# Scores of keys ahead of scores of queries in the first chunk of a delta-rule attention with a feed-forward block

## The chip, the core and the metric

The kernel runs on one core of a Trainium2 chip. The core has TensorE (PE; its loading of weights is listed as PEld), VectorE (DVE), ScalarE (ACT), GpSimd (POOL) and SyncE (SP), which issues all of this kernel's DMAs. The metric is the time of one execution on the device in microseconds. Before the change it is 787.22 us, the median of three runs (784.6, 787.22, 788.08).

## What is computed

A delta-rule attention over 4 batches, 8 heads, 768 steps and a head dimension of 48, and then a feed-forward block with SiLU on the 3072 tokens:

```python
k_n = k / (np.linalg.norm(k, axis=-1, keepdims=True) + 1e-06)
for t in range(S):
    y[:, :, t] = np.einsum('bhd,bhde->bhe', q[:, :, t], state)
    v_old = np.einsum('bhde,bhd->bhe', state, kt)
    state = state + bt[:, :, :, None] * np.einsum('bhd,bhe->bhde', kt, vt - v_old)
...
h = x @ w_in                              # x: the attention's output, (3072, 384); w_in: (384, 2048)
g = h * (1.0 / (1.0 + np.exp(-h)))
out = g @ w_out                           # w_out: (2048, 384)
```

The weights come as 64-bit floats and are made into 32-bit floats on the chip.

## The kernel before, in words

The 768 steps are cut into six chunks of 128. A unit is one batch of one chunk, with all 8 heads; each chunk has four units. Within a chunk the recurrence is written as a triangular system: the scores between the keys, times the step sizes, form a triangular matrix per head, and its inverse gives the values that are really added to the state.

For one chunk, the steps are these. `squares` and `norms` (L284, L301) make the step sizes g from the norms of the keys and beta. `turn` (L353) transposes k and q of a unit on PE into the tile kq; ACT copies the transposes from PSUM (L371 for k, L369 for q, with a factor of -1). `score` (L376) multiplies the transposed keys with keys and queries together (L387, 256 columns: 128 of keys and 128 of queries). The results go into the tile ap, scaled by g; the part of the queries is also masked with the triangle `above`. ACT evicts some heads (L397), DVE the others together with the mask (L403). `block_out` (L415) writes the 32 x 32 diagonal blocks of the key scores to DRAM with four DMAs per unit, and `block_in` (L435) reads them back with one head's block per partition, into the tile g. `invert` (L441) is the substitution: DVE makes the inverses of all 128 blocks, one row after another, by pairs of instructions at L465 and L469, each of which reads two SBUF tiles. When it is done (L473 on ACT, L474 on DVE), the blocks go out to DRAM as `up` and `low` (L480) and come back in pieces (L490). `solve` (L508) merges the blocks (`merge`, L540, evicted at L548, L549 and L545, L546), applies them to the values (L572, L580; sums at L563, copies at L590, L595), updates the state and makes the attention's output xT (L650, L662). `feed_forward` (L867) then runs over the chunk: `hidden` (L720) with w_in, `project` (L744) or, from the second chunk on, `combine` (L806) with w_out.

The first chunk, chunk 0, has no feed-forward work to lie beside it. In its place the weights are made narrow: `narrow` (L150) takes a piece of 768 KB and needs two ACT instructions (L158, L163), three DVE instructions (L160, L166, L170) and an addition on POOL (L174). `fetch_w_in` (L192) and `fetch_w_out` (L219) load the pieces. `fill(n)` (L936) emits the next n steps of this, in a fixed queue: eight pieces of w_in, then eight of w_out. `busy` (L261) emits matmuls whose result nobody uses.

The order on each engine is the order in which the program emits instructions: `pin` (L88) ties each instruction to the one before it on its engine, and `in_line` (L98) does the same for the DMAs of SP's queue. So an instruction that waits holds up all that follow on its engine. PSUM has three pools, psA and psC with three banks and psM with two.

The part that the change touches is L142 to L145 (first loads: beta, k of the four units, q of the four units), and L878 to L1007 (the written-out order of chunk 0). There, before the change, q is loaded behind k; `turn` and `score` of each unit run whole, one unit after another; POOL makes bkb (L340) and, after the substitution, scales the values (L348). While DVE does the substitution (the loop at L959), beta of the other chunks is transposed, the loads named in `ORDER` are emitted, k and q of chunk 1 are transposed at the steps named in `TURN`, and 20 `busy` follow. After the loop the loads of `REST` are emitted, `squares(1)` and `norms(1)`, then `fill(3)`, and the solve of chunk 0 begins, with some `busy` behind its first steps.

Of the kernel before, what the change touches and what calls it, by code (L numbers as in the profile page):

```python
# [10 lines left out]
FP32 = mybir.dt.float32  # L11
# [10 lines left out]
def kernel(  # L22
# [51 lines left out]
    def bank(pool, tag, name):  # L74
        return pool.tile([P, 512], FP32, name=name, tag=tag)
# [22 lines left out]
    def in_line(dma):  # L98

        if line:  # L100
            behind(dma, line[-1])
        line.append(dma)
        return dma
# [36 lines left out]
    pin(nc.vector.memset(states[B - 1][:], 0.0))  # L140
    beta_fm = mlp.tile([BH, S], FP32, name="beta_fm", tag="gT", bufs=3)
    in_line(nc.sync.dma_start(out=beta_fm[:], in_=beta.rearrange("b h s -> (b h) s")))  # L142
    for load_one in (load_k, load_q):
        for i in range(B):
            load_one(i)  # L145
    w_in = const.tile([P, NKT, DFF], FP32, name="w_in")
    HFF = NFF // 2
    w_outs = [const.tile([P, HFF, DM], FP32, name=f"w_out{i}") for i in range(2)]
# [43 lines left out]
    def fetch_w_in(i):  # L192
        if i < 4:
            raw = room(1 - i // 2, i % 2)
        elif i < NWI - 1:
            raw = mlp.tile([P, SIZE], U32, name="raw", tag="gT", bufs=3)[:]
        else:
            raw = spare
        raw = raw.rearrange("p (a f) -> p a f", a=NKT)
        src = moe_w_in.rearrange("(a p) f -> p a f", p=P)[:, :, i * WF : (i + 1) * WF].bitcast(U32)  # L200
        in_line(nc.sync.dma_start(out=raw, in_=src))
        raws["in", i] = raw.rearrange("p a (f j) -> p a f j", j=2)
# [58 lines left out]
    def busy(after=None, how=NoSync):  # L261

        pw = bank(psC, "c", "pw")
        done = pin(nc.tensor.matmul(
            pw[:, 0:DM], lhsT=ident[:],
            rhs=states[B - 1][:].rearrange("p a w -> p (a w)")[:, 0:DM], start=True, stop=True,
        ))
        if after is not None:
            behind(done, after, how)
        return done  # L270
# [13 lines left out]
    def squares(c):  # L284

        sums[c] = small.tile([P, BH], FP32, name="ss", bufs=1)[:]
        for b in range(B):
            if c == 1:
                sq = packed(zbufs[b])
            else:  # L290
                if b % HB == 0:
                    two = work.tile([P, HB, H, D], FP32, name="sq", tag="g" if c > 0 else "xg"[b // HB], bufs=1)
                sq = two[:, b % HB]
            pin(nc.scalar.activation(
                out=sq, in_=packed(kbufs[(c * B + b) % NK]), func=ACTF.Square
            ))
            pin(nc.vector.tensor_reduce(
                out=sums[c][:, b * H : (b + 1) * H], in_=sq, axis=AX.X, op=ALU.add
            ))
# [53 lines left out]
    def turn(i, *rooms):  # L353

        b, c = units[i]
        kb, qb = kbufs[i % NK], zbufs[i % NZ]
        kq = work.tile([P, NP, 2, C], FP32, name="kq", bufs=4)
        u = dict(kq=kq, bkb=bkbufs[i % NBK])
        for j, (src, room) in enumerate(zip((kb, qb), rooms)):
            if j == 1:  # L360
                yield u
            pt = bank(*room, "pt")
            for p in range(NP):
                pin(nc.tensor.transpose(  # L364
                    pt[:, p * C : (p + 1) * C], src[:, p].rearrange("p e w -> p (e w)"), ident[:]
                ))
            ptv = pt[:].rearrange("p (a t) -> p a t", a=NP)
            if j == 1:
                pin(nc.scalar.mul(kq[:, :, j, :], ptv, -1.0))  # L369
            elif c <= 1:  # L370
                pin(nc.scalar.copy(kq[:, :, j, :], ptv))  # L371
            else:
                pin(nc.vector.tensor_copy(out=kq[:, :, j, :], in_=ptv))
        yield u

    def score(i, u, rooms):  # L376
# [5 lines left out]
        for g, room in enumerate(rooms):  # L382
# [29 lines left out]
            u["ends"] = (copied, masked)  # L412
            yield

    def block_out(i, u):  # L415

        b, c = units[i]
        ap = u["ap"]
        if b == 0:
            blocks[c] = (  # L420
                tc.dram_tile([B, H, NB, T, T], FP32, name=f"blocks{c}"),
                work.tile([P, T, T], FP32, name="g", tag="g", bufs=1),
                work.tile([P, T, T], FP32, name="x", tag="x", bufs=1),
            )
            x = blocks[c][2]
            pin(nc.gpsimd.memset(x[:], 0.0))  # L426
            pin(nc.gpsimd.memset(x[:].rearrange("p s t -> p (s t)")[:, 0 : T * T : T + 1], 1.0))
        there = blocks[c][0]
        for j in range(NB):
            rows = slice(T * j, T * (j + 1))  # L430
            in_line(nc.sync.dma_start(  # L431
                out=there[b, :, j].rearrange("h s t -> s h t"), in_=ap[rows, :, 0, rows]
            ))

    def block_in(i):  # L435
        b, c = units[i]
        there, g, _ = blocks[c]
        rows = slice(T * b, T * (b + 1))
        in_line(nc.sync.dma_start(out=g[rows], in_=there[b].rearrange("h j s t -> (h j) s t")))

    def invert(c):  # L441

# [432 lines left out]
                yield from project(c, b, o)  # L875


    ORDER, TURN, REST = {1: (2, 3, "q", "v", 4)}, (5, 7, 9, 11), (5, 6, 7)  # L878
    A, CC, M = (psA, "a"), (psC, "c"), (psM, "m")

    def go(steps, n=1):
        for _ in range(n):
            next(steps, None)
# [19 lines left out]
    for _ in range(3):  # L903
        busy()
    squares(0)
    turning = [turn(b, M, M) for b in range(2)]
    us = [next(t) for t in turning]
    beta_of(0)
    for t in turning:
        next(t)  # L910
    norms(0)
    for b in range(B):
        if b >= 1 and b + 1 < B:
            us.append(list(turn(b + 1, M, M))[0])
        go(score(b, us[b], (CC, A)), 3)
        block_out(b, us[b])
        if b > 0:
            block_in(b - 1)
    block_in(B - 1)
    for b in range(B):  # L920
        scale(b)
    for i in range(B, 2 * B):
# [36 lines left out]
    for n, done in enumerate(invert(0)):  # L959
        if n == 1:  # L960
            for c in range(1, NCH):
                beta_of(c)
        for of in ORDER.get(n, ()):
            if of == "q":
                for i in range(B, 2 * B):
                    load_q(i)
            elif of == "v":
                for i in range(B):
                    load_v(i)
            else:  # L970
                fetch_w_in(of)
        if n in TURN:
            next_us.append(list(turn(B + len(next_us), M, M))[0])
        if n == 18:
            for i in range(20):
                busy(done if i == 0 else None, Sync)
    for i in REST:
        fetch_w_in(i)
    squares(1)
    norms(1)  # L980

    def until(piece):
        while piece is not None and piece not in narrowed:
            fill(1)
# [4 lines left out]
        fetch_w_out(i)  # L989

    fill(3)
    for i in (0, 1, 4):
        more(i, ("in", 1))
    for b in range(B):
# [2 lines left out]
    for n, _ in enumerate(solve(0, us)):  # L997
        fill(2)
        if n == 3:
            more(2)  # L1000
            more(3)
        if n == 8:
            more(5, ("out", 1))
        for _ in range((3, 3, 2, 2, 1, 1, 1)[n] if n < 7 else 0):
            busy()
        if n >= 7:
            go(pieces, 2)  # L1007
# [91 lines left out]
```

## Time and profile before

| what | number |
|---|---|
| median of three runs | 787.22 us |
| the profiled execution's own time | 784.6 us |
| its span, first to last instruction | 782.7 us |
| mean granted TensorE clock | 0.973 |
| PE busy over the span | 94% |
| DVE busy over the span | 53% |
| substitution of chunk 0 on DVE (L456 to L469) | 31.58 to 53.98 us |
| POOL's idle time ahead of L174 at 62.08 | 33.4 us |
| first matmul of the feed-forward part (L726) | 91.84 us |

A row of the timeline gives the start, the duration, the engine, the line and operation, the output and inputs with their shapes, and the number of merged instructions; in brackets stands the idle time before it and what ended that. A row of the windows gives, for a stretch, its length, the busy time of PE, PEld, DVE, ACT and POOL with the number of instructions, then the granted clock of PE, the share of the DMA engines, and GB/s. The granted clock is 1.00 or 0.50 in most stretches of the first 100 us: 1.00 from 10 to 30, 0.50 from 35 to 45, 1.00 from 50 to 75 and 0.50 from 80 to 85. A load of k or q of a unit (192 KB) takes 1.2 us of a full DMA queue, at about 163 GB/s; a piece of w_in (768 KB) 2.0 us, at about 390 GB/s.

### The profile page before, as it was taken

What the parts mean: (1) busy time and instruction counts of PE and PEld (TensorE: products, weight loads), DVE (VectorE), ACT (ScalarE), POOL (GpSimd) and SP (SyncE); (2) the same over time, 40 slices, a digit from 0 to 9 for tenths busy, and PEclk for the clock granted to TensorE, in tenths of its full rate; (3) what the DMA queues carried; (4) which work ended last, traced back from release to release, by engine and by line L of the source; (5) the groups of instructions that cost most, each with busy time, mean ns of one, the idle gap of its engine ahead of it and who ended that gap; (6) DMA issues with size and microseconds to landing.
All of it is one profiled execution on the core that took longest, in us unless ns stands there. A gap on an engine that the chain in (4) does not pass through costs nothing.

```text
span 782.7 us, 16587 instructions
## 1 busy us (share of the span) xinstructions
PE 736.8 (94%) x6806; PEld 635.1 (81%) x6806; DVE 411.9 (53%) x1050; ACT 227.3 (29%) x492; POOL 83.6 (11%) x95
## 2 busy tenths in 40 slices
PE   7389899999999799999899999899999999999998
PEld 5255786677877799988799998799998899998987
DVE  6889697852543753544572446492454592321212
ACT  6445475121233122324112315112314202212020
POOL 4006347000003000003000003000003000000000
PEclk9779899999999899999899999999999999999999
DMA  9888353130126022026213025303025203010000
GB/s 173 162 181 243 123 169 71 37 95 10 30 62 122 18 81 36 15 57 128 41 48 68 8 56 113 65 20 96 3 49 109 41 21 95 5 30 29 21 1 21
DMA packets 161723, 53.88 MB, mean 69 GB/s; under 512 B 143440, under 2 KB 154192, under 8 KB 161648
## 3 DMA queue, kind: packets, MB, share of 16 engines
q1 hardware_dynamic: 161648, 52.82, 29.5%
q8 instruction: 54, 0.88, 0.5%
q14 instruction: 21, 0.17, 0.1%
HBM read 34.70 MB, written 14.16 MB: 62 GB/s over the span
## 4 chain that ended last, share of the span: by engine, by line
PE 57%; SPq 5%; DMA 4%; issue 1%; ACT 0%; DVE 0%; ACTq 0%; DVEq 0%
PE phid L726 18%; PE px L820 14%; PE py L820 10%; DMA blocks<-ap 3%; PE pz L572 3%; PE pyc L632 2%; SPq L431 2%; PE pyc L604 2%; PE ph L556 2%; SPq L675 2%; PE pa L387 2%; PE py L540 1%; PE px L540 1%; PE pu L615 1%; PE pt L364 1%
## 5 line engine op out<-in xcount | busy, mean ns | idle before, releaser
L726 PE MATMUL phid<-xT,w_in 128*128 128x256 f32 x1152 | 260.7, 382 | 2.2 <-ACT gT L736 1.6
L726 PEld LDWEIGHTS phid<-xT,w_in 128*128 128x128 f32 x1152 | 214.8, 190 | 37.2 <-issue 6.3
L736 ACT ACTIVATE gT<-phid 128x512 f32<-128x512 f32 x96 | 56.9, 597 | 180.5 <-PE phid L726 160.2
L403 DVE SCALAR_TENSOR_TENSOR ap<-pa,g,above 128x128 f32<-128x128 f32 x192 | 58.1, 376 | 41.9 <-ACT ap L397 41.9
L469 DVE TENSOR_TENSOR x<-x,rank 128x30 f32<-128x30 f32 (+9 forms) x180 | 59.7, 331 | 7.4 <-ACT x L458 1.1
L465 DVE TENSOR_TENSOR rank<-g,x 128x30 f32<-128x30 f32 (+9 forms) x180 | 59.5, 330 | 5.0
L802 DVE TENSOR_TENSOR sums_of_g<-gT 128x384 f32<-128x384 f32 (+1 forms) x60 | 29.3, 510 | 55.7 <-ACT gT L736 45.2
L820 PE MATMUL py<-w_out,sums_of_g 128*128 128x192 f32 x320 | 57.0, 329 | 0.4 <-DVE o L828 0.4
L820 PE MATMUL px<-sums_of_w,sums_of_g 128*128 128x192 f32 x320 | 56.8, 329 | 0.0
L820 PEld LDWEIGHTS px<-sums_of_w,sums_of_g 128*128 128x128 f32 x320 | 52.2, 190 | 1.4 <-issue 1.4
L820 PEld LDWEIGHTS py<-w_out,sums_of_g 128*128 128x128 f32 x320 | 52.1, 190 | 1.3 <-DVE o L828 0.7
L426 POOL MEMSET x<- 128x1024 f32 x6 | 5.7, 952 | 432.7 <-DMA xT<-part 431.3
L397 ACT ACTIVATE ap<-pa,g 128x128 f32<-128x128 f32 x144 | 41.6, 368 | 30.7 <-PE pa L387 29.7
L387 PE MATMUL pa<-kq 48*128 48x256 f32 x384 | 49.8, 390 | 0.2 <-DVE ap L403 0.2
L749 PE MATMUL po<-w_out,gT 128*128 128x384 f32 x128 | 44.7, 495 | 2.9 <-POOL w_out L174 2.9
L820 PE MATMUL px<-w_out,gT 128*128 128x192 f32 x160 | 35.1, 378 | 13.1 <-ACT gT L736 13.0
L572 PEld LDWEIGHTS pz<-vf,xi 64*64 64x64 f32 x768 | 38.0, 141 | 10.3 <-issue 7.3
L387 PEld LDWEIGHTS pa<-kq 48*128 48x128 f32 x384 | 36.2, 186 | 11.7 <-issue 7.9
L572 PE MATMUL pz<-vf,xi 64*64 64x48 f32 x768 | 42.6, 227 | 2.0 <-DVE vf L563 1.6
L820 PEld LDWEIGHTS px<-w_out,gT 128*128 128x128 f32 x160 | 31.9, 224 | 15.2 <-ACT gT L736 14.7
L590 ACT COPY z<-pz 64x384 f32<-64x384 f32 x48 | 22.6, 472 | 63.8 <-PE pz L572 54.7
L563 DVE TENSOR_TENSOR vf<-vf,ph 128x384 f32<-128x384 f32 x20 | 11.1, 555 | 53.2 <-PE ph L556 53.2
(133 smaller groups left out, 905.3 us busy)
## 6 DMA issues: line engine op xcount, KB each, us to landing
kb<-in_k_dram SPq DMA_DIRECT2D x24, 192.0 KB, 3.1
z<-in_q_dram SPq DMA_DIRECT2D x24, 192.0 KB, 3.2
vf<-in_v_dram SPq DMA_DIRECT2D x24, 192.0 KB, 4.0
out_dram<-o SPq DMA_DIRECT2D x24, 192.0 KB, 2.0
w_out<-in_moe_w_in_dram SPq DMA_DIRECT2D x4, 768.0 KB, 6.4
blocks<-ap SPq DMA_DIRECT2D x96, 32.0 KB, 2.2
g<-blocks SPq DMA_DIRECT2D x24, 128.0 KB, 2.5
up<-x SPq DMA_DIRECT2D x6, 512.0 KB, 2.6
```

The source lines that it names most:

```text
L387: u["last"] = pin(nc.tensor.matmul(pa[e][:, pp * 2 * C : (pp + 1) * 2 * C], lhsT=kq[rows, 2 * g + pp, 0, :], rhs=kq[rows, 2 * g + pp, :, : ...
L397: copied = pin(nc.scalar.activation(out=ap[:, h, 0, :], in_=pa[e][:, at : at + C], func=ACTF.Copy, scale=bt[:, h : h + 1],))
L403: masked = pin(nc.vector.scalar_tensor_tensor(out=ap[:, h, j:2, :], in0=pa[e][:, at + j * C : at + 2 * C].rearrange("p (j t) -> p j t", j= ...
L465: pin(nc.vector.tensor_tensor(out=tv, in0=g[:, 0:m, m : m + 1].to_broadcast([P, m, n]), in1=x[:, m : m + 1, m + 1 : T].to_broadcast([P, m, ...
L469: yield pin(nc.vector.tensor_tensor(out=x[:, 0:m, m + 1 : T], in0=x[:, 0:m, m + 1 : T], in1=tv, op=ALU.add))
L572: yield pin(nc.tensor.matmul(pzs[x][rows, h, :], lhsT=xis[x // HB][rows, x % HB * H + h, :], rhs=vs[x][rows, h, :], start=True, stop=True,))
L590: pin(nc.scalar.copy(z_of(x)[rows, :, :, 0:D], pzs[x][rows].rearrange("p (a e) d -> p a e d", e=2)))
L726: pin(nc.tensor.matmul(ph[:, j * GT : (j + 1) * GT], lhsT=w_in[:, a, (2 * f + j) * P : (2 * f + j + 1) * P], rhs=xTs[c, hf][:, a, :], star ...
L736: pin(nc.scalar.activation(out=gTs[f // FG][:, f % FG, :], in_=ph[:], func=ACTF.Silu, scale=0.5))
L749: pin(nc.tensor.matmul(po[:, 0:DM], lhsT=gTs[f // 2 // FG][:, f // 2 % FG, at : at + C], rhs=w_outs[f // HFF][:, f % HFF, :], start=(f == ...
L802: pin(nc.vector.tensor_tensor(out=sums_of_g[:, k, fs], in0=of[0], in1=of[1], op=op))
L820: pin(nc.tensor.matmul(to, lhsT=at, rhs=quarter(f, *b) if isinstance(b, tuple) else sums_of_w[b][:, f], start=start and f == 0, stop=f == ...
```

## The change

In chunk 0 the scores are made in two parts by a new function, `score_part`. The part of the keys (j = 0) is made for all four units as soon as the step sizes are there, from the transposes of k alone. The loads of q of the first four units move behind the blocks in SP's queue. The blocks of two units are read back by one DMA. The part of the queries (j = 1) is made inside the substitution, at the steps 5, 7, 9 and 11 (`SECOND`): transposes of q, matmuls, eight ACT evictions per unit, and one POOL multiplication with the triangle in place of DVE's masking. The transposes of chunk 1 come at later steps, those of its queries behind the loop. w_in 4 is fetched behind the substitution with 5, 6 and 7. Of the `busy` ahead of the merges 9 are left of 20, and the first two steps of the solve have four in place of three. `squares(1)` and `norms(1)` move behind `fill(3)`.

```diff
-    for load_one in (load_k, load_q):
-        for i in range(B):
-            load_one(i)
+    for i in range(B):
+        load_k(i)
...
+    def score_part(i, u, j, room):
+
+        b, c = units[i]
+        kq, bt = u["kq"], steps[c][:, b * H : (b + 1) * H]
+        if j == 0:
+            u["ap"] = work.tile([P, H, 2, C], FP32, name="ap", tag="ap", bufs=4)
+        ap = u["ap"]
+        pa = [bank(*room, f"pa{e}") for e in range(2)]
+        for p in range(NP):
+            for e in range(2):
+                rows = slice(W * e, W * e + D)
+                pin(nc.tensor.matmul(
+                    pa[e][:, p * C : (p + 1) * C], lhsT=kq[rows, p, 0, :], rhs=kq[rows, p, j, :],
+                    start=True, stop=True,
+                ))
+        for e in range(2):
+            if j == 0 and (e == 1 or b == B - 1):
+                pin(nc.vector.tensor_tensor(
+                    out=ap[:].rearrange("p (a e) j t -> p a e j t", e=2)[:, :, e, 0, :],
+                    in0=pa[e][:].rearrange("p (a t) -> p a t", a=NP),
+                    in1=bt.rearrange("p (a e) -> p a e", e=2)[:, :, e].unsqueeze(2).to_broadcast([P, NP, C]),
+                    op=ALU.mult,
+                ))
+                continue
+            for p in range(NP):
+                h = 2 * p + e
+                pin(nc.scalar.activation(
+                    out=ap[:, h, j, :], in_=pa[e][:, p * C : (p + 1) * C], func=ACTF.Copy,
+                    scale=bt[:, h : h + 1],
+                ))
+        if j == 1:
+            pin(nc.gpsimd.tensor_tensor(
+                out=ap[:, :, 1, :], in0=ap[:, :, 1, :],
+                in1=above[:].unsqueeze(1).to_broadcast([P, H, C]), op=ALU.mult,
+            ))
...
-    def block_in(i):
+    def block_in(i, n=1):
...
-        rows = slice(T * b, T * (b + 1))
-        in_line(nc.sync.dma_start(out=g[rows], in_=there[b].rearrange("h j s t -> (h j) s t")))
+        rows = slice(T * b, T * (b + n))
+        in_line(nc.sync.dma_start(
+            out=g[rows], in_=there[b : b + n].rearrange("b h j s t -> (b h j) s t")
+        ))
...
-    ORDER, TURN, REST = {1: (2, 3, "q", "v", 4)}, (5, 7, 9, 11), (5, 6, 7)
+    ORDER, SECOND = {4: (2,), 8: (3,), 12: ("q", "v")}, (5, 7, 9, 11)
+    TURN, REST = (14, 17, 20, 23), (4, 5, 6, 7)
...
-    turning = [turn(b, M, M) for b in range(2)]
+    turning = [turn(b, M, CC) for b in range(B)]
     us = [next(t) for t in turning]
     beta_of(0)
-    for t in turning:
-        next(t)
     norms(0)
     for b in range(B):
-        if b >= 1 and b + 1 < B:
-            us.append(list(turn(b + 1, M, M))[0])
-        go(score(b, us[b], (CC, A)), 3)
+        score_part(b, us[b], 0, (A, CC, M, A)[b])
         block_out(b, us[b])
-        if b > 0:
-            block_in(b - 1)
-    block_in(B - 1)
+        if b == HB:
+            block_in(0, HB)
+    block_in(HB, HB)
+    for i in range(B):
+        load_q(i)
...
+        if n in SECOND:
+            b = SECOND.index(n)
+            next(turning[b])
+            score_part(b, us[b], 1, (A, CC)[b % 2])
         if n in TURN:
-            next_us.append(list(turn(B + len(next_us), M, M))[0])
+            turning.append(turn(B + len(next_us), M, M))
+            next_us.append(next(turning[-1]))
         if n == 18:
-            for i in range(20):
-                busy(done if i == 0 else None, Sync)
+            late = done
+    for t in turning[B:]:
+        next(t)
+    for i in range(9):
+        busy(late if i == 0 else None, Sync)
     for i in REST:
         fetch_w_in(i)
-    squares(1)
-    norms(1)
...
     fill(3)
+    squares(1)
+    norms(1)
...
-        for _ in range((3, 3, 2, 2, 1, 1, 1)[n] if n < 7 else 0):
+        for _ in range((4, 4, 2, 2, 1, 1, 1)[n] if n < 7 else 0):
             busy()
```

## The prediction

> **What bounds the kernel now.** I read the page first, then the timeline of each engine over the first 160 us, because every line of the diff acts before about 80 us (queue SP, then DVE, ACT, POOL, PE), then the windows of 5 us, and the waits of SP.
>
> ```profile
> PE 736.8 (94%) x6806; PEld 635.1 (81%) x6806; DVE 411.9 (53%) x1050; ACT 227.3 (29%) x492; POOL 83.6 (11%) x95
> ```
>
> PE is 94% busy, but up to 60 us part of that is `busy` matmuls (L264), which compute nothing. The first matmul of the feed-forward part (L726) starts at 91.84. What decides when that happens is a chain of small steps: scores of the keys, their blocks out to DRAM and back (SP), the substitution (DVE), its result out and back, the solve. From 92 us on the engines follow their written-out orders without a free stretch of any size, so I count a shift of this chain in full. SP's queue and DVE show the chain:
>
> ```profile
> 16.26 4.21 SPq L431 DMA_DIRECT2D blocks<-ap  x8
> 20.65 0.32 SPq L439 DMA_DIRECT2D g<-blocks  x1
> 22.05 1.78 SPq L431 DMA_DIRECT2D blocks<-ap  x4
> 23.95 0.38 SPq L439 DMA_DIRECT2D g<-blocks  x1
> 24.43 3.10 SPq L431 DMA_DIRECT2D blocks<-ap  x4
> 27.64 1.49 SPq L439 DMA_DIRECT2D g<-blocks  x2
> ```
> ```profile
> 12.74 0.19 DVE L326 SCALAR_TENSOR_TENSOR g<-nr,nt 128x32 f32<-128x32 f32 x1
> 13.76 4.88 DVE L403 SCALAR_TENSOR_TENSOR ap<-pa,g,above 128x128 f32<-128x128 f32 x16 [0.83 <-ACT ap L397]
> 19.55 4.76 DVE L403 SCALAR_TENSOR_TENSOR ap<-pa,g,above 128x128 f32<-128x128 f32 x16 [0.92 <-ACT ap L397]
> ...
> 31.58 0.36 DVE L456 COPY x<-g 128x16 f32<-128x16 f32 x3 [2.38 <-DMA g<-blocks]
> 31.86 0.20 DVE L465 TENSOR_TENSOR rank<-g,x 128x30 f32<-128x30 f32 x1
> ```
>
> The step sizes g are there at 12.93. DVE then spends 2 x 4.8 us on 32 evictions, up to 24.31, and the last unit's blocks leave SP at 24.43 to 27.53. They are read back by an issue that ends at 29.13, and the substitution starts at 31.58. Its last instruction ends at 53.98; call that moment E. After E come `up` and `low` out (54.04 and 55.18), their pieces back, and the merges.
>
> Of the three engines beside DVE, POOL matters: between 28.64 and 62.08 it does nothing. What happens when POOL and DVE both read SBUF is seen a little later:
>
> ```profile
> 69.54 2.02 POOL L174 TENSOR_TENSOR w_in<-w_in,w_out 128x768 int32<-128x768 int32 x1
> ...
> 70.16 2.22 DVE L170 SCALAR_TENSOR_TENSOR w_in<-w_out,w_in 128x768 uint32<-128x768 uint32 x1
> ```
>
> L170 alone takes 0.95; here it ends at 72.38, 0.82 after POOL's end at 71.56. It stood still until POOL was done. L403, which reads PSUM and one tile of SBUF, kept its 0.3 each beside POOL's L340 at 13.02 to 16.21.
>
> **The change, step by step.** Numbers with E are counted from the end of the substitution.
>
> 1. Key scores first. k stays first in SP's queue, so the sums of squares, the norms and g at 12.93 stay. The transposes and copies of k2 and k3 move ahead of beta's copy on ACT (9.58 now): two copies of 0.53 with their transposes put it at about 11.4. L325 needs it at 12.51, so it is hidden; later than that it would cost one to one. Score matmuls of 128 columns are not in the trace. L387 with 256 columns takes 2.0 per unit, half the columns give 1.0 to 2.0; PE makes all of it while waiting for g, so either end costs nothing.
> 2. Evictions. ACT does 4 x 0.277 (1.66 for 6 at 13.03) = 1.1 per unit, DVE one instruction of 512 elements, between 0.56 (L563, 384 elements from PSUM) and four of L403 (1.2): I take 0.7, off the path beside ACT. Unit 0 is ready at 13.03 + 1.1 = 14.15 in place of 16.2.
> 3. SP. Each block issue costs 0.445 (1.78 for 4). Units 0 to 2: 14.2 to 19.6. The first double read: 0.4, to 20.0. Unit 3: to 21.8, its last issue at 21.35, landing 1.7 later (the median of these DMAs) at 23.1. The second double read is issued there and lands as now 2.7 later, plus an estimated 0.3 for twice the bytes: 26.2. The substitution starts at 26.2 in place of 31.58: **-5.4**. Bounds -4.4 (SP waits again at each unit) and -6.
> 4. The q loads move past w_in 0 and 1, 16 block issues and two reads. q0 lands about 26.7 (3.2 after issue, like k0). The loads of q4 to q7 and v now wait behind the transposes of q0 to q3, into the forties; v is first used by POOL's L348 after E, so that is hidden.
> 5. Scores of the queries in the substitution. ACT, per unit: 0.6 (L369), a wait for PE, 8 x 0.277 = 2.2. PE's part is 1.6 to 2.7 by its clock (PEclk is 0.50 in 35 to 45 us now). So 4.7 to 5.8 per unit, four units from 28.6 to 47 or 52, then four k copies to 50 or 55. Before E, if E stays late.
> 6. The masks: four POOL instructions of 1024 elements, one at the end of each unit, so at about 34, 39, 44 and 50: in the middle of the substitution. L340, a float multiplication, takes 0.83 for 384 elements, which gives 2.2; L174 (1.84 for 768) gives 2.45; a POOL memset of 1024 takes 0.95. I take **2.2**. L465 and L469 read two SBUF tiles each, back to back, on the path. No row shows them beside POOL. From one side this costs nothing, from the other the whole POOL instruction. The nearest row is L170, which also reads two SBUF tiles and was stopped completely. So I take 4 x 2.2 = **+8.8**, ends 0 and 9.8.
>
> The Trainium skill, "SBUF — State Buffer", section "Who interferes with whom", speaks against this step: it says that `tensor_tensor` with both inputs in SBUF contends with GpSimd's reads, and that the one that comes second waits for the whole instruction of the first. The L170 row agrees (2.22 for 0.95); no row shows L465. By that rule the four masks cost 8.8, by a reading in which only L170's kind of instruction is stopped they cost 0.
>
> So E moves by -5.4 + 8.8 = **+3.4**, to about 57.4.
>
> 7. After E. w_in 4 was issued at 45.57; now it stands behind all pieces of `up` and `low`, at E + 11.8, where w_in 5 was. Raw pieces land 5.9 after issue: E + 17.7. ACT's L158 for it ran at E + 13.7 (67.64), and behind it in ACT's order stands L545, which ran at E + 15.4 and now comes at E + 18.6. PE: four transposes of q wait for ACT's L369 (ACT's L473 is ahead of them), then 9 `busy` at 0.65 and four in place of three before each of the next two merges; the third merge (68.14, E + 14.2) comes at E + 17 at full clock, E + 19.5 at half. Against that, DVE has little idle time here:
>
> ```profile
> 60.00:65.00 5.00, 4.61 (x83) 2.68 (x83) 4.80 (x9) 1.49 (x2) 2.92 (x3) 1.00 0.59 95
> 65.00:70.00 5.00, 5.00 (x134) 3.60 (x133) 4.91 (x5) 3.01 (x5) 5.00 (x5) 1.00 0.86 213
> 70.00:75.00 5.00, 5.00 (x107) 3.53 (x105) 4.89 (x5) 2.82 (x5) 3.40 (x2) 1.00 1.04 352
> 75.00:80.00 5.00, 3.12 (x65) 2.36 (x64) 4.84 (x7) 2.52 (x5) 1.91 (x1) 0.84 1.02 401
> ```
>
> The third busy column is DVE: 4.8 to 4.9 of 5 up to 80 us. The first new value of z that everyone waits for is added by L563 at 77.99 (E + 24.0), in DVE's order, 2.6 after PE had it. So the lateness on ACT and PE is mostly swallowed. DVE gets a gap of about 3 before Abs of w_in 2, but POOL's L174 and L348 now run in that gap and not against L166, L170 and L160, which saves 1.3 + 0.3 + 0.6. I get +0.4 with PE at full clock, +2.4 at half, and take **+1.5**.
>
> Sum: 3.4 + 1.5 = **+4.9**. Against the profiled execution (784.6, its span 782.7 plus 1.9 around it) that is 789.5. The three runs are 784.6, 787.22 and 788.08; the profiled one is the fastest, so I add the shift to the median, 787.2: **792.1**.
>
> **Rivals.** (a) The masks stop DVE, but cheaply: a mask takes nearer 2, one falls outside the substitution, the swallowing is complete. Then -5.4 + 6.6 to 8.2 + 0.4, so +1.6 to +3.2: about 789.6, within 0.5% (3.9 us, about what a measurement of this kernel can tell from no change). For it: four masks hit only if ACT's units are finished before E. (b) Not slower: POOL does not stop L465 and L469, or waits for gaps that DVE doesn't give. The place is the 22.4 us of the substitution, the price of step 6 goes to 0, and E would be at 48.6. But then ACT decides: L473 stands behind the q units and k copies, 50 to 55 in place of 54.07. That leaves -4.3 to +1, and with +0.5 after E about -3: 784.2, and 782.9 at best. It decides as soon as a mask costs DVE under 1 us. Against it: the L170 row. (c) The early part gives nothing, because SP still waits at each unit or the w_in transfers, now issued at 4.2, hold the blocks up: -5.4 becomes -3, and the time 794.5. Against it: DMA stands at 390 GB/s when w_in moves, so both pieces are in by 13, before the first block.
>
> **How the numbers follow.** Forecast with (c): 0.52, own range 791 to 796. (a): 0.24. (b): 0.24, of which 0.15 beyond 0.5% and 0.09 inside. So faster 0.15, same 0.33, slower 0.52. The range runs from the fast end of (b) with -6 in place of -5.4 at the start (-4.9), 782.3, to the sum with (c)'s -3, 2.45 per mask and half clock (-3 + 9.8 + 2.4 = +9.2), 796.4.
>
> **What would show it.** L456 starting near 26 shows steps 1 to 3. POOL rows of about 2.2 at the mask's line, with L465 or L469 beside them at 2.4 to 2.6 in place of 0.3 to 0.4, show step 6; unchanged rows there make me wrong, towards (b). E near 57 and L726 first at 96 to 98 show the sum. ACT's L158 waiting for raw from DMA, with L545 behind it, shows step 7; L563 first at E + 24 to 26 shows how much was swallowed.

## The result, and the profile after

The changed kernel takes 796.42 us (median of 4 runs, 792.5 to 796.97), the kernel before 786.92 in runs beside it (median of 4, 784.6 to 788.08). The ratio is 1.0114, with a 95% interval of 1.0074 to 1.0154: slower by about 9 us, where +4.9 was forecast. The profiled execution took 796.97 us, its span is 795.0. Lines behind the new function are shifted: L456, L465, L469 and L473 of before are now L493, L502, L506 and L510, L563 is L600, L726 is L763, L736 is L773.

The page's busy times have hardly moved, except POOL's, which has four instructions and 8.8 us more:

```profile
PE 737.1 (93%) x6852; PEld 638.0 (80%) x6852; DVE 413.5 (52%) x1023; ACT 231.8 (29%) x512; POOL 92.4 (12%) x99
```

SP's queue in the timeline of the changed kernel (start, duration, what is issued):

```profile
14.28 6.62 SPq L466 DMA_DIRECT2D blocks<-ap  x12
21.07 0.53 SPq L474 DMA_DIRECT2D g<-blocks  x1
21.64 2.07 SPq L466 DMA_DIRECT2D blocks<-ap  x4
25.57 0.47 SPq L474 DMA_DIRECT2D g<-blocks  x1
```

The first block issue is where it was forecast, at 14.28. The first twelve take 6.62, which is 0.55 each on average and not 0.445; one of them takes 1.30. The issue of the last read begins at 25.57, 2.5 later than forecast, and ends at 26.04 (before 29.13). DVE and POOL in the same timeline:

```profile
29.19 0.36 DVE L493 COPY x<-g 128x16 f32<-128x16 f32 x3 [7.08 <-DMA g<-blocks]
...
36.38 0.39 DVE L502 TENSOR_TENSOR rank<-g,x 128x220 f32<-128x220 f32 x1
36.81 2.42 DVE L506 TENSOR_TENSOR x<-x,rank 128x220 f32<-128x220 f32 x1
...
41.44 2.57 DVE L506 TENSOR_TENSOR x<-x,rank 128x238 f32<-128x238 f32 x1
...
46.26 2.58 DVE L506 TENSOR_TENSOR x<-x,rank 128x238 f32<-128x238 f32 x1
...
51.46 2.42 DVE L502 TENSOR_TENSOR rank<-g,x 128x210 f32<-128x210 f32 x1
53.91 0.38 DVE L506 TENSOR_TENSOR x<-x,rank 128x210 f32<-128x210 f32 x1
...
60.10 0.60 DVE L511 COPY g<-x 128x512 f32<-128x512 f32 x1
```
```profile
36.57 2.41 POOL L445 TENSOR_TENSOR ap<-ap,above 128x1024 f32<-128x1024 f32 x1 [15.01 <-ACT ap L440]
41.40 2.35 POOL L445 TENSOR_TENSOR ap<-ap,above 128x1024 f32<-128x1024 f32 x1 [2.42 <-ACT ap L440]
46.23 2.35 POOL L445 TENSOR_TENSOR ap<-ap,above 128x1024 f32<-128x1024 f32 x1 [2.48 <-ACT ap L440]
51.05 2.59 POOL L445 TENSOR_TENSOR ap<-ap,above 128x1024 f32<-128x1024 f32 x1 [2.48 <-ACT ap L440]
```

Each mask has one substitution instruction beside it that takes 2.42 to 2.58 where its neighbours take 0.38 to 0.41. Each of these ends within 0.3 of its mask. The excess is 2.03 + 2.16 + 2.17 + 2.04 = 8.4 us. The substitution now runs from 29.19 to 60.07: 30.9 us in place of 22.4.

After that moment E, the first `vf` addition (L600) is at 85.48 = E + 25.4 (before E + 24.0), but the first gT eviction (L773), the copy out of PSUM of the feed-forward part's first product, is at 100.66 = E + 40.6 (before 94.79 = E + 40.8); the two rows before the change, and the two after:

```profile
77.99 0.56 DVE L563 TENSOR_TENSOR vf<-vf,pz 64x384 f32<-64x384 f32 x1
94.79 0.60 ACT L736 ACTIVATE gT<-phid 128x512 f32<-128x512 f32 x1 [1.27 <-PE phid L726]
```
```profile
85.48 0.56 DVE L600 TENSOR_TENSOR vf<-vf,pz 64x384 f32<-64x384 f32 x1
100.66 0.60 ACT L773 ACTIVATE gT<-phid 128x512 f32<-128x512 f32 x1 [1.28 <-PE phid L763]
```

What was late was made up. The windows show a likely reason (the third busy column is DVE; of the last three numbers the first is the granted clock):

```profile
75.00:80.00 5.00, 5.00 (x79) 3.17 (x76) 4.72 (x6) 3.41 (x5) 2.34 (x2) 1.00 1.01 363
80.00:85.00 5.00, 5.00 (x118) 3.74 (x116) 4.42 (x6) 2.54 (x5) 2.60 (x2) 1.00 1.05 403
85.00:90.00 5.00, 3.33 (x58) 1.93 (x54) 4.73 (x6) 4.67 (x9) 2.53 (x2) 1.00 0.55 214
```

In the kernel before, the clock was 0.84 in 75 to 80 and, in the row behind it,

```profile
80.00:85.00 5.00, 3.55 (x55) 2.27 (x52) 2.82 (x4) 2.38 (x5) 1.83 (x1) 0.50 0.09 33
```

TensorE ran that stretch at half clock before, and at full clock now. So 5.9 us of lateness reach the feed-forward part. At the last gT eviction it is 12.2 in these two traces: the rest came in the later chunks, which the change does not touch. That was not in the forecast.

### The profile page after: what moved, and what is told of

It is laid out like the page before. It is cut to its first block, busy times and chain, and to the rows that moved or that the text cites. A ratio compares the mean times of both kernels' runs of the same rounds, so it can differ in the third digit from the quotient of the medians.

```text
span 795.0 us, 16651 instructions
## 1 busy us (share of the span) xinstructions
PE 737.1 (93%) x6852; PEld 638.0 (80%) x6852; DVE 413.5 (52%) x1023; ACT 231.8 (29%) x512; POOL 92.4 (12%) x99
## 4 chain that ended last, share of the span: by engine, by line
PE 58%; DMA 4%; SPq 3%; POOL 1%; ACT 1%; issue 1%; DVE 0%; ACTq 0%; DVEq 0%
PE phid L763 19%; PE px L857 14%; PE py L857 10%; PE pz L609 3%; DMA blocks<-ap 2%; PE pa L386 2%; PE ph L593 2%; PE pyc L669 2%; PE pyc L641 2%; SPq L466 2%; PE py L577 1%; PE px L577 1%; PE pt L363 1%; PE pu L652 1%; DMA kb<-in_k_dram 1%; PE pz L617 1%
## 5 line engine op out<-in xcount | busy, mean ns | idle before, releaser
L763 PE MATMUL phid<-xT,w_in 128*128 128x256 f32 x1152 | 260.7, 382 | 2.2 <-ACT gT L773 1.7
L763 PEld LDWEIGHTS phid<-xT,w_in 128*128 128x128 f32 x1152 | 214.8, 190 | 37.2 <-issue 6.3
L773 ACT ACTIVATE gT<-phid 128x512 f32<-128x512 f32 x96 | 56.9, 598 | 180.4 <-PE phid L763 150.1
L506 DVE TENSOR_TENSOR x<-x,rank 128x30 f32<-128x30 f32 (+9 forms) x180 | 66.1, 367 | 7.4 <-ACT x L495 1.1
L402 DVE SCALAR_TENSOR_TENSOR ap<-pa,g,above 128x128 f32<-128x128 f32 (+1 forms) x160 | 48.5, 376 | 40.2 <-ACT ap L396 40.1
L502 DVE TENSOR_TENSOR rank<-g,x 128x30 f32<-128x30 f32 (+9 forms) x180 | 61.5, 342 | 5.0
L857 PE MATMUL px<-w_out,gT 128*128 128x192 f32 x160 | 38.0, 401 | 15.5 <-ACT gT L773 15.5
L857 PEld LDWEIGHTS px<-w_out,gT 128*128 128x128 f32 x160 | 34.6, 240 | 17.6 <-ACT gT L773 17.2
L396 ACT ACTIVATE ap<-pa,g 128x128 f32<-128x128 f32 x120 | 34.6, 365 | 28.6 <-PE pa L386 28.6
L386 PE MATMUL pa<-kq 48*128 48x256 f32 x320 | 40.9, 390 | 0.0
L600 DVE TENSOR_TENSOR vf<-vf,ph 128x384 f32<-128x384 f32 x20 | 11.1, 555 | 53.1 <-PE ph L593 53.1
L786 PEld LDWEIGHTS po<-w_out,gT 128*128 128x128 f32 x128 | 23.3, 190 | 18.4 <-POOL w_out L173 4.1
```

Source lines behind the costliest of these rows:

```text
L386: u["last"] = pin(nc.tensor.matmul(pa[e][:, pp * 2 * C : (pp + 1) * 2 * C], lhsT=kq[rows, 2 * g + pp, 0, :], rhs=kq[rows, 2 * g + pp, :, : ...
L396: copied = pin(nc.scalar.activation(out=ap[:, h, 0, :], in_=pa[e][:, at : at + C], func=ACTF.Copy, scale=bt[:, h : h + 1],))
L402: masked = pin(nc.vector.scalar_tensor_tensor(out=ap[:, h, j:2, :], in0=pa[e][:, at + j * C : at + 2 * C].rearrange("p (j t) -> p j t", j= ...
L502: pin(nc.vector.tensor_tensor(out=tv, in0=g[:, 0:m, m : m + 1].to_broadcast([P, m, n]), in1=x[:, m : m + 1, m + 1 : T].to_broadcast([P, m, ...
L506: yield pin(nc.vector.tensor_tensor(out=x[:, 0:m, m + 1 : T], in0=x[:, 0:m, m + 1 : T], in1=tv, op=ALU.add))
L763: pin(nc.tensor.matmul(ph[:, j * GT : (j + 1) * GT], lhsT=w_in[:, a, (2 * f + j) * P : (2 * f + j + 1) * P], rhs=xTs[c, hf][:, a, :], star ...
```

## The experiments

Each is a ratio to the kernel before, run on the same chip; in brackets its 95% interval. Kernels of one chip shared its runs: e1 to e4 (before 785.8, 20 runs), e5 to e8 (782.07, 23 runs), e9 to e11 (783.6, 23 runs), e12 (784.15, 17 runs).

**The masks: e1 to e5.** e1 is the changed kernel, timed again.

> The changed kernel once more, nothing edited, for a second trace and more times. In the first trace the shift against the kernel before was 5.9 us at the first eviction of the feed-forward part, 6.1 at the third chunk and 12.2 at the end. If the part behind chunk 0 is chance (cold windows of TensorE and slow block transfers that fall differently in each execution), this trace shows 5.7 to 6.1 again at the first eviction (100.4 to 100.9 us), but another shift at the end, anywhere from 3 to 13. If the change itself costs something in later chunks, the end is again 11 to 13 late.

Measured: 795.23 (6 runs), 1.0124 [1.0088, 1.0160]. Substitution from 29.11 to 59.99; lateness 6.4 at the first gT eviction, a little over the 5.7 to 6.1 expected, and 9.3 at the last one. So what comes on top behind chunk 0 was 6.3 in the first trace and 2.9 in this one of the same kernel, and a good part of it differs from execution to execution.

e2 is the changed kernel with L445 left out; it leaves out the masking of the query scores in chunk 0.

```
-        if j == 1:
-            pin(nc.gpsimd.tensor_tensor(out=ap[:, :, 1, :], in0=ap[:, :, 1, :],
-                in1=above[:].unsqueeze(1).to_broadcast([P, H, C]), op=ALU.mult))
```

> The changed kernel without the four POOL multiplications: the scores of the queries of chunk 0 stay unmasked, that part of the computation is left out. If the masks stop VectorE (they stretched four of its instructions by 2.0 to 2.2 us each, 8.4 in all), the substitution lasts 22.4 us in place of 30.9, ends near 51.7, and the first eviction of the feed-forward part comes 8 us earlier, near 92.5; the time is 786 to 789, level with the kernel before. Rival: ScalarE's queue then decides (its last copy of a k transpose ended at 53.3), and 1 to 2 of the 8 are lost: 94, and 788 to 790. Rival: the loss lies in the order behind the substitution and the time stays over 793.

Measured: 787.15 (10 runs), 1.0021 [1.0000, 1.0041]. The substitution takes 22.5 us again (29.40 to 51.85), with no long instruction in it. The masks are worth 795.23 - 787.15 = 8.1 us, between 5 and 11 by the intervals (1.0124 and 1.0021, each with 0.2 to 0.4% either way). E is 2.1 earlier than before, yet the first gT eviction is at 95.01 against 94.79: it was expected at 92.5, and the rival that ScalarE's queue decides had 94. The time was within the 786 to 789 expected. ACT shows why the early end is not passed on; the copy that starts the steps after E, in e2 and in the kernel before:

```profile
54.25 1.11 ACT L505 COPY g<-x 128x512 f32<-128x512 f32 x1
55.23 1.12 ACT L368 ACTIVATE kq<-pt 128x512 f32<-128x512 f32 x2
```
```profile
54.07 1.09 ACT L473 COPY g<-x 128x512 f32<-128x512 f32 x1 [5.31 <-DVE x L469]
```

In e2 the copy waits 2.4 us behind ACT's score and key copies and comes no earlier than before. Even with free masks the early start would have ended there.

e3 is the kernel before with four multiplications of the masks' size on POOL, which compute nothing; e4 has memsets in their place.

```
+        if n in (6, 11, 16, 21):
+            behind(pin(nc.gpsimd.tensor_tensor(out=sum_room[:, 0 : H * C]...,
+                in0=above[:]..., in1=above[:]..., op=ALU.mult)), done, Sync)
...
+            behind(pin(nc.gpsimd.memset(sum_room[:, 0 : H * C], 0.0)), done, Sync)
```

> The kernel before with one thing added: four POOL multiplications of 1024 elements that read two SBUF tiles and write a scratch area, at the steps 6, 11, 16 and 21 of the first substitution, where POOL does nothing else. If POOL's reading stops VectorE's instructions with two SBUF inputs, four of the substitution's instructions take 2.2 to 2.6 us, its end moves by 8 to 9.6 from 54.0 to 62 to 63.6, and the time is 794 to 797. If they run side by side, nothing moves: 786 to 788.

> The same place and size, but four POOL memsets, which only write. If it is POOL's reading that stops VectorE, the substitution keeps its 22.4 us and ends at 54.0. If any POOL instruction does, four instructions are stretched by about 0.9 each and it ends near 57.6.

Measured: e3 793.54 (7 runs), 1.0100 [1.0068, 1.0132]; e4, a single run, 785.49. In e3 E moves by 6.1 to 60.04, where 8 to 9.6 was expected. POOL's and DVE's rows in e3, the first two of the four:

```profile
35.40 2.04 POOL L973 TENSOR_TENSOR sums_of_w<-above 128x1024 f32<-128x1024 f32 x1 [6.83 <-DVE x L469]
41.01 2.04 POOL L973 TENSOR_TENSOR sums_of_w<-above 128x1024 f32<-128x1024 f32 x1 [3.57 <-DVE x L469]
```
```profile
35.72 1.91 DVE L469 TENSOR_TENSOR x<-x,rank 128x168 f32<-128x168 f32 x1
...
41.33 1.97 DVE L469 TENSOR_TENSOR x<-x,rank 128x228 f32<-128x228 f32 x1
```

POOL's instructions alone, with nothing else of the change, bring the same kind of stop: four of 1.91 to 1.98 us, beside POOL's 2.00 to 2.05. In e4 no DVE instruction of the substitution is stretched, and it takes 22.4 us:

```profile
38.73 0.95 POOL L973 MEMSET sums_of_w<- 128x1024 f32 x1 [3.08 <-DVE x L469]
```

So in these runs it is POOL's reading of SBUF that stops DVE, not its running. The Trainium skill, "SBUF — State Buffer", section "Who interferes with whom", says this too: a VectorE instruction with two SBUF inputs contends with a GpSimd instruction that reads SBUF, not with one that only writes it. Both halves are now measured on this kernel.

e5 masks with one SBUF input in place of two.

```
-            pin(nc.gpsimd.tensor_tensor(out=ap[:, :, 1, :], in0=ap[:, :, 1, :], in1=above..., op=ALU.mult))
+            pin(nc.gpsimd.affine_select(out=ap[:, :, 1, :], in_=ap[:, :, 1, :], pattern=[[0, H], [1, C]],
+                compare_op=ALU.is_gt, fill=0.0, base=0, channel_multiplier=-1))
```

> The changed kernel with the triangle masked by POOL's affine_select, which reads one SBUF tile in place of two. If POOL's reading is what stops VectorE, each mask still costs its whole duration, but that duration is shorter: by the 0.29 us of the 128-element select at the start, an estimate of 1.0 to 2.0 us for 1024 elements, so the substitution lasts 26.5 to 30.4 us in place of 30.9 and the time is 788 to 795. If only a POOL instruction with two SBUF inputs stops VectorE, the substitution keeps 22.4 us and the time is 786 to 789.

Measured: 785.28 (10 runs), 1.0046 [1.0010, 1.0082]. The substitution takes 25.9 us, a little under the 26.5 to 30.4 expected. POOL's and DVE's first rows:

```profile
36.24 1.16 POOL L445 TENSOR_SCALAR_AFFINE_SELECT ap<-ap 128x1024 f32<-128x1024 f32 x1 [14.98 <-ACT ap L440]
41.05 1.09 POOL L445 TENSOR_SCALAR_AFFINE_SELECT ap<-ap 128x1024 f32<-128x1024 f32 x1 [3.65 <-ACT ap L440]
```
```profile
36.49 1.15 DVE L506 TENSOR_TENSOR x<-x,rank 128x220 f32<-128x220 f32 x1
...
41.18 1.22 DVE L502 TENSOR_TENSOR rank<-g,x 128x240 f32<-128x240 f32 x1
```

A POOL instruction with one SBUF input stops DVE just as fully, but for 1.1 us and not 2.4: the four stops cost 0.76 + 0.81 + 0.90 + 0.92 = 3.4.

**The early start: e8.** The changed kernel with each unit's blocks read back by themselves, as before the change.

```
-        if b == HB:
-            block_in(0, HB)
-    block_in(HB, HB)
+        if b > 0:
+            block_in(b - 1)
+    block_in(B - 1)
```

> The changed kernel with the blocks read back unit by unit, as before the change. A read of 128 KB landed in 2.6 us, one of 256 KB in 3.6. If the double read costs that, the substitution starts 0.7 to 1 us earlier, at 28.2 to 28.5, and everything behind it follows. If the start is set by the last unit's blocks alone, it stays at 29.1 to 29.4. The masks are untouched, so the time is 793 to 796 in both cases.

Measured: 790.79 (4 runs), 1.0123 [1.0080, 1.0166]. SP's last read leaves by 25.1 and the substitution starts at 27.44, earlier than either case expected, so the double reads cost 1.7 (against e1, which like e8 begins its blocks at 13.9 to 14.0: 0.7 in SP's queue, 1.0 in the reading).

```profile
27.44 0.36 DVE L493 COPY x<-g 128x16 f32<-128x16 f32 x3 [5.64 <-DMA g<-blocks]
```

E is at 58.25. But the first gT eviction comes at 103.20 = E + 44.9: nothing is won. That TensorE's clock is the cause is not shown, but it is the visible difference (0.50 is the clock in both rows):

```profile
60.00:65.00 5.00, 5.00 (x14) 3.48 (x15) 1.63 (x2) 4.02 (x8) 5.00 (x6) 0.50 0.57 176
...
90.00:95.00 5.00, 5.00 (x88) 4.85 (x85) 3.29 (x6) 1.38 (x4) 0.35 (x1) 0.50 0.01 3
```

In the changed kernel the clock from 65 to 100 is 1.00 throughout.

**The lateness in the later chunks: e6, e9, e10, e12.** Comparing SP's queue, I saw single issues that came 1.1 to 1.9 us behind the one before, among others 0.45 to 0.6 apart. Most of those behind the first chunk follow, by 1.3 to 1.9 us, a packet of this queue of the page:

```profile
q8 instruction: 54, 0.88, 0.5%
```

These are 16 KB each, 54 of them over 6852 + 6852 TensorE records: 254 records a packet. In the records of the DMA queues such a packet mostly took 0.9 to 1.4 us, and 1.9 at most in the kernel before. A packet goes by the count of TensorE instructions, so most pauses stand at the same DMA in every run with the same stream of TensorE instructions: at issues 124, 147, 214, 303 and 392 in the kernel before, e3 and e4, and at 120, 131, 210, 223, 299, 310, 386 and 398 in the changed kernel and e1. The change adds 46 matmul records and 46 weight loads (23 matmuls of the program), which moves all later pauses. SP in the same stretch (the next chunk's `xT` transfers, then its blocks) before and after:

```profile
588.64 6.23 SPq L675 DMA_DIRECT2D xT<-part  x10
...
608.93 1.85 SPq L431 DMA_DIRECT2D blocks<-ap  x4
```
```profile
595.29 7.52 SPq L712 DMA_DIRECT2D xT<-part  x10
...
616.70 3.24 SPq L466 DMA_DIRECT2D blocks<-ap  x4
```

The two groups with a pause take 1.3 and 1.4 longer. In this trace TensorE then runs dry before the next chunk and loses its clock; the windows of 620 to 640, before and after:

```profile
620.00:630.00 10.00, 10.00 (x63) 10.00 (x63) 9.26 (x26) 0.89 (x3) 0.00 (x0) 1.00 0.01 2
630.00:640.00 10.00, 9.60 (x57) 9.09 (x56) 9.52 (x26) 0.26 (x1) 0.00 (x0) 1.00 0.00 0
```
```profile
620.00:630.00 10.00, 6.97 (x31) 5.97 (x30) 2.19 (x12) 2.28 (x5) 0.00 (x0) 0.89 0.22 46
630.00:640.00 10.00, 10.00 (x49) 10.00 (x48) 9.38 (x26) 0.82 (x2) 0.00 (x0) 0.77 0.00 1
```

In e1, the same kernel once more, the third group of blocks takes 1.86 without a pause, TensorE is idle there for less, and the clock stays at 1.00:

```profile
620.00:630.00 10.00, 8.32 (x42) 7.25 (x41) 2.80 (x13) 2.28 (x5) 0.00 (x0) 1.00 0.17 39
630.00:640.00 10.00, 10.00 (x63) 10.00 (x62) 9.38 (x26) 1.15 (x3) 0.00 (x0) 1.00 0.00 1
```

e6 is the kernel before with 23 small matmuls where TensorE is idle at 25 us, e10 the same with 64 (128 records of each kind: a whole packet); e9 is the changed kernel with 41 more (23 + 41 = 64), e12 is e2 with 41 more, ahead of the nine `busy`.

```
+    for of in (8, 8, 7):
+        pw = bank(psC, "c", "pw")
+        for _ in range(of):
+            pin(nc.tensor.matmul(pw[:, 0:2], lhsT=ident[:], rhs=states[B - 1][:, 0, 0:2], ...))
...
+    for of in (14, 14, 13):
+            pin(nc.tensor.matmul(pw[0:T, 0:T], lhsT=ident[0:T, 0:T], rhs=ident[0:T, 0:T], ...))
```

> The kernel before with 23 more matmuls of 2 columns on TensorE at 25 us, where TensorE is idle for 6.7 us: as many more instructions in TensorE's stream (two weight loads and two matmuls each) as the change adds. Nothing else differs. The traces show pauses of 0.8 to 1.4 us in SP's queue, each 1.3 to 1.9 us behind a 16 KB packet of the instruction queue, at the same DMA of the list in every run of one kernel, and at others in the changed kernel. If the place of these packets is set by the count of TensorE instructions, here the pauses move to where the changed kernel has them (chunk 4 to 5: near the third group of xT pieces and the third group of blocks), the first eviction of the feed-forward part stays at 94.8 to 95.4, and the end comes 2 to 4 us later: 788 to 790. If the later loss is chance, the time stays at 785 to 787.

> The changed kernel with 41 more matmuls of 32 x 32 on TensorE at 18 us, where it is idle. 64 matmuls fill one 16 KB packet of TensorE's instructions (54 packets for 6,806 matmuls and as many weight loads); the change added 23, so with 41 more the packets fall at the same work of the later chunks as in the kernel before. If the place of the packets costs the changed kernel what 23 matmuls cost the kernel before (0.6%, 4.7 us), the ratio falls from 1.012 to 1.005 to 1.008, with the substitution as it was (29.1 to 60.1 us). If not, it stays at 1.011 to 1.014.

> The kernel before with 64 more matmuls of 32 x 32 at 25 us: a whole packet more. If it is the place of the packets that cost 0.6% with 23 more matmuls, the place is the same again and the ratio is 0.998 to 1.003. If more instructions as such cost it, the ratio is 1.006 or more.

> The changed kernel without its four masks (this leaves out the masking of the query scores in chunk 0) and with 41 matmuls of 32x32 in TensorE's stream just ahead of the nine `busy` matmuls, where TensorE waits for the substitution to end. With the 23 that the change adds this makes 64, the number after which SP's pauses lie as in the kernel before. Without the 41 this kernel took 1.0021 of the time before. If the position of TensorE's instruction packets is what takes the 2 us of the early start back in the later chunks: the pauses at about the DMA issues of the kernel before (124, 147, 232, 303, 348, 392, 478), the shift of the gT evictions no larger at the end than at the first one (it was +0.2 and then +3.6), and a ratio of 0.997 to 0.9995. If the position is not what costs: pauses moved, but a ratio of 1.001 to 1.003 as without the 41, with the shift growing by about 3 again. If the start of the substitution or the clock behind it differs from 29.4 and 0.956, the early part is told apart by the first eviction (95.0).

Measured: e6 786.75 (12 runs), 1.0058 [1.0031, 1.0084]; e10 784.38 (12 runs), 1.0018 [0.9989, 1.0047]. 23 matmuls of two columns cost 0.6%, and 64 of 32 x 32 nothing that can be told from no change, though the two intervals overlap. The pauses were where expected in both. The first gT eviction of e6 was not: it came at 93.64 and not at 94.8 to 95.4. The kernel before has a packet at 24.19 and behind it a block issue of 1.62; in e6 the packet comes at 21.08, the issue takes 0.37, and the substitution starts at 30.12 in place of 31.58. e9: 792.95 (6 runs), 1.0118 [1.0078, 1.0158], a miss. The pauses lay as before the change, and the lateness grew by only 1.4 behind the first gT eviction, but that eviction came at 104.74, with half clock in 60 to 65 and 90 to 95. e12: 787.66 (12 runs), 1.0042 [1.0014, 1.0069], a miss as a ratio too. Its 41 matmuls stood behind transposes that wait for ACT, and so held TensorE up for 2.78 us ahead of the first merge; the first gT eviction came at 97.78 and not 95.01. Behind it the lateness grew by 1.1 where e2's grew by 3.3.

Since each trace has its own early part, I take that out: time against before (ratio less 1, times before's median) less the shift of the first gT eviction against 94.79.

| TensorE records added | kernels | time, us | first gT, us | left for the later chunks, us | the same, by the profiled execution's own time |
|---|---|---|---|---|---|
| 46 | after, e1 | +9.0, +9.7 | +5.9, +6.4 | +3.1, +3.4 | +4.2, +1.9 |
| 46 | e2, e5 | +1.7, +3.6 | +0.2, +1.8 | +1.4, +1.8 | +2.3, -1.0 |
| 46 | e6, e8 | +4.5, +9.6 | -1.2, +8.4 | +5.7, +1.2 | +4.4, +0.2 |
| 0 | e3, e4 | +7.9, -0.3 | +7.5, +0.6 | +0.3, -0.9 | +0.9, -0.9 |
| 128 | e9, e10 | +9.2, +1.4 | +10.0, +2.2 | -0.7, -0.8 | +2.5, -3.4 |
| 128 | e11, e12 | -1.7, +3.3 | -1.2, +3.0 | -0.5, +0.3 | -3.8, +1.5 |
| 64 | e7 | +8.1 | +8.7 | -0.7 | +0.3 |

By the medians all six entries with 46 added records lose 1.2 to 5.7 us in the later chunks, and the six with none or a whole packet lie between -0.9 and +0.3. But that column takes an eviction of one trace from a median of other executions. The last column takes time and eviction from the same execution, and there the two groups overlap: -1.0 to +4.4 against -3.8 to +2.5. The interval of a time alone is 1.6 to 3.4 us either way, the 94.79 is of a single trace (e4, which differs by four memsets, has 95.39), and e7, whose packets are displaced by half a packet, loses nothing. So it is shown that the pauses follow the packets and move with the count of instructions; that they cost the changed kernel its 3 us in the later chunks is not shown.

**Other places for the query scores: e7 and e11.** e7 is the kernel before with key scores first and the query scores directly behind, ahead of the substitution; DVE masks half of the heads while reading PSUM, POOL the other half. e11 is e7 with all q copies ahead of the scores, POOL's half by `affine_select`, and 32 small matmuls more, which make up the packet.

```
+    for b in range(B):
+        next(turning[b])
+        score_part(b, us[b], 1, (A, M)[b % 2])
...
+    for b in range(B):
+        next(turning[b])
+    for b in range(B):
+        score_part(b, us[b], 1, (A, M)[b % 2])
```

> The kernel before with the scores of the keys first, and those of the queries directly behind them, ahead of the substitution: q is loaded where it was, half of the heads are evicted by VectorE with the mask from PSUM, half by ScalarE and masked by POOL while the blocks travel; the reads of the blocks, the order behind the substitution and all other loads are as before. The substitution should start at 28.5 to 30 us and last 22.4, so end at 51 to 52.5 in place of 54.0, and the first eviction of the feed-forward part come 1.5 to 3 us earlier: 783 to 785. If the early start is given back behind the substitution, as without masks (0.2 late there although its substitution ended 2.1 early), the time is 786 to 788.

> The scores of the keys first and those of the queries ahead of the substitution, as in the earlier run, with what held that one up taken away: all four copies of q ahead of the scores, bkb made ahead of them, ScalarE's half masked by affine_select, and 32 small matmuls to make the change of TensorE's stream a whole packet. There DVE started the substitution at 37.9, although the blocks had been read back at 28. Now it should start at 28.5 to 30.5 and end at 51 to 53 in place of 54.0; the ratio is 0.994 to 0.999. If TensorE's clock drops between the scores and each unit takes 3.8 us as there, the start is 33 to 36 and the ratio 1.002 to 1.006.

Measured: e7 790.27 (6 runs), 1.0103 [1.0061, 1.0144], a miss. A unit of query scores takes 3.8 us (ACT, then PE at half clock, then ACT), and the substitution stands behind them and behind w_in work in DVE's order. It starts at 37.89 and lasts 23.8. e11: 782.37 (12 runs), 0.9978 [0.9952, 1.0004]. DVE in e11:

```profile
28.72 0.34 DVE L501 COPY x<-g 128x16 f32<-128x16 f32 x3
...
51.15 0.61 DVE L519 COPY g<-x 128x512 f32<-128x512 f32 x1
```

As expected, the substitution starts 2.9 earlier than before and keeps its 22.4 us. This version is level with the kernel before, or faster by up to 0.5%, and clearly faster than the changed one.

## Why the prediction was right, and where not

The direction was right and so was the reason for it; the size was half. That 796.42 still lies at the end of the widest range (782.3 to 796.4), just past the 791 to 796 given for the forecast itself, is in part luck: that end was summed as -3 + 9.8 + 2.4, and what came was -2.4 + 8.4 - 0.2 and some 3 us from a part of the kernel that the sum took as unchanged. By the steps of the prediction:

- **Steps 1 and 2** held: the first block issue came at 14.28 (forecast 14.2).
- **Step 3** failed in size: -2.4 in place of -5.4, outside its bounds of -4.4 and -6. That is near the -3 of rival (c), by another cause: SP did not wait at each unit. The first twelve block issues took 6.62 in place of 5.4, with one issue of 1.30 behind an instruction packet at 14.9, and the first read 0.53 in place of 0.4; the last blocks landed 2.2 behind their issue in place of 1.7, behind the first double read (24.82). So the last read was issued at 25.57 and not at 23.1, 2.5 late. The start of 31.58 that the shift is counted from has a packet in it too: the kernel before started at 30.12 in e6, where the packet fell elsewhere. From there to the start it took 3.6 and not 3.0: I gave 0.3 for twice the bytes, and the double reads cost more. With single reads (e8) the start is 1.7 earlier.
- **Step 4** held in what counts: between 26 and 62 no engine's wait is put down to a load of q or v. But q of the first unit landed at 30.30 and not at 26.7.
- **Steps 5 and 6** held: units of 4.83 on ACT (forecast 4.7 to 5.8), four masks, all inside the substitution, 8.4 us against +8.8. e2 and e3 show it from both sides. So (b) falls, and (a) with its cheaper masks, though only just (6.6 to 8.2 against 8.4); its complete swallowing did come. What (b) said of ACT was right: without masks the copy behind E waits for ACT and comes at 54.25 (e2). The "about -3" of (b) does not follow from its own bounds: -4.3 to +1 and +0.5 have their middle near -1.2, and e2 measured +0.2 at the first gT eviction. The page on SBUF that step 6 quotes does not "speak against" it, as it puts it, but says what the step assumes.
- **E** was forecast at +3.4 and came at +6.1; the difference is step 3's.
- **Step 7**: the first addition came 1.4 later behind E (forecast 1.5), but not for the named reasons alone. ACT did not wait for raw at w_in 4; the merges stood behind the nine `busy` matmuls (6.50 us from 63.50). The first matmul of the feed-forward part (L726, now L763) began at 97.71, inside the 96 to 98 named as a sign, although E was 2.7 later than forecast. What was lost was given back, most likely by the full clock, so that E to the first gT eviction took 40.6 against 40.8. That the two agree is in part luck. Over the five runs with the changed order behind E and the masks inside (after, e1, e5, e8, e9) this stretch took 40.6 to 44.9, with half clock from about 90 to 97 in the two longest; over the seven that keep the order of before it took 40.8 to 42.5. The term of 1.5 was smaller than this spread.
- **The shift counted in full** from 92 us on. It did, but about 3 us came on top in the later chunks (+3.1 and +3.4 in the table by the medians). I had looked at no resource that depends on the count of instructions, and nothing in the sum stood for such a loss.

So the sum is -2.4 + 8.4 = 6.0 (E: 6.1), -0.2 to the first gT eviction, +3 in the later chunks: 9, as measured. That the masks are the largest term is shown (e2, e3). Where those 3 come from stays open: the packets, TensorE's clock falling otherwise, or both. In the changed kernel itself the time did not come down with the pauses back in place (e9); in its one trace the early part was worse by as much.

## What to carry to other kernels

Work that is moved beside another engine's critical chain is not free because its own engine is idle: look whether both read SBUF (here POOL, and VectorE with two SBUF inputs), and charge POOL's whole instruction on the chain for each overlap. Where POOL must work beside such a chain, take a form that reads less (1.1 us for 2.4), or let the engine that evicts PSUM apply the mask, as L403 does before the change (0.3 each, also beside POOL). A chain that is made shorter ends at the next engine in line; here ACT's queue would have taken all of the 2.1 us, even without the masks (e2).

## What was not expected of the hardware

- TensorE's instructions come as DMA packets, 16 KB for about 254 records, and behind many of them SP's queue stood still for 0.8 to 1.4 us. Adding 23 tiny matmuls in idle time cost 0.58% [0.31, 0.84]; adding 64, 0.18% [-0.11, 0.47]. The Trainium skill, "Runtime: NRT & Kernel Launch", section "Instruction fetch mechanics", gives blocks of 16 KiB with 256 instructions, which agrees with the 254. It calls the cost of crossing such a block mostly hidden; the delay of SP's issues behind a packet is not hidden in these traces.
- The stretches of half clock are 3.4, 6.8 or more in multiples of 3.4 us long, and fall differently from kernel to kernel, in the later chunks also from one execution to the next (the changed kernel and e1). With 6.8 us of it from about 90 on, the stretch from E to the first gT eviction was 3.4 to 4.4 us longer than in the changed kernel (e9, e8). That this is its cause is not shown; an early gain of 1.7 us vanished there (e8).
